# An attention-then-FFN kernel on one core: its head re-ordered (beta later, turn parts in own PSUM banks, dummy matmuls, a queue of squares, four begun FFN1 units)

## The chip, the cores and the metric

The kernel runs on one core of a Trainium2 chip. Its time is the device time of one execution in microseconds; the figure compared is the median of several runs. The profile is of one such execution. PE is TensorE, PEld its weight loads, DVE VectorE, ACT ScalarE, POOL GpSimd and SP SyncE, which here only starts transfers.

## What is computed

```
scores = q @ k^T / sqrt(64)                     # per batch (8) and head (12), 448 x 448
attn   = max(scores, 0)^2 / 448
x      = (attn @ v), heads side by side         # 3584 x 768
h      = x @ w_in                               # 3584 x 2048
g      = max(h, 0) + alpha * min(h, 0)
out    = g @ w_out                              # 3584 x 768, float32
```

Inputs are float32; the matmuls run in bf16.

## The kernel before, in words

Work is tiled by **quad**: four heads of one batch, so three quads (NG = 3) per batch and 24 in all. For each quad:

- `load_qk`, `load_v` (lines 86 to 99) bring q, k and v from HBM as bf16 through POOL's queue. The first quad's q and k come as float32 instead, on SP's and ACT's queues (lines 114 to 117), and are cast by DVE and ACT (line 123).
- `turn_pe` (133) transposes q and k with 14 PE transposes each into a PSUM bank (line 141) and copies them into tile `T` (144 on DVE, 146 on ACT). For the first quad the copy is cut into two parts for each of q and k. From quad 6 on `turn_dma` (149) is used: DVE permutes, a DMA transposes.
- `score_mm` (161) makes one of seven chunks j of scores: four matmuls of 64x64 weights and 448 columns, one for each quarter of the array, into a pair of banks (line 166).
- `relu` (172) takes a chunk out of PSUM as `rl`, on ACT (175) or DVE (177); the letter for each chunk is in the pattern string. `square` (180) multiplies `rl` by itself on DVE into `at` (182).
- `attnv` (185), A@V, accumulates seven squared chunks against v (28 matmuls, line 192) and writes the result, scaled, as `xT`: one half by ACT (199), one by DVE (200).

The FFN follows: `f1` (227) makes one of 16 units ff of a batch, six matmuls of 448 columns (215), then ACT makes `neg` = relu(-h) (223) and DVE gT = h + (1 - alpha) * neg (224), with `beta_sb` = 1 - alpha (line 128). `f2` (232) makes an output tile with 16 matmuls of 384 columns (237); ACT copies it out (239) and SP stores it.

The order of work on every engine is the order in which this Python code issues instructions: the schedule is manual, each engine runs its own list in order, and semaphores join them. PSUM is one tile of eight banks; `take_bank` and `take_pair` give the bank or the pair that was taken longest ago, and dependencies through PSUM are by bank. `rl` has 7 buffers, `at` 12, `neg` 3.

The head, lines 253 to 286, interleaves quads 0, 1 and 2 by hand in calls of `run`, which issues a group of score chunks with their relus and then all squares of the group. FFN1 of batch 0 then begins with two units begun on their first four matmuls (those that need only quads 0 and 1) before A@V of quad 2. Lines 300 to 327 mix FFN1 of batch 0, the scores of quads 3 to 5, and the first FFN2 units (which lack batch 1 and so take only c below 3). At line 349 two FFN1 units of batch 1 are begun ahead of A@V of quad 5. `burst` (338) is the later pattern: three chunks, A@V of an earlier quad, three chunks, then squares.

## Time and profile before

| what | value |
|---|---|
| median of 14 runs | 398.73 us (397.14 to 400.15) |
| the profiled execution | 397.89 us, span 396.1 us |
| PE busy | 376.2 us, 95% of the span |
| DVE busy | 265.7 us, 67% |
| ACT busy | 207.4 us, 52% |
| first 28 us: PE / DVE / ACT busy | 14.2 / 17.5 / 16.8 us |
| 28 to 73 us: PE / DVE / ACT busy | 42.7 / 33.4 / 28.2 us |
| 73 to 140 us: PE / DVE / ACT busy | 67.0 / 47.4 / 35.4 us |
| moved by DMA in the first 28 us | 190 GB/s |

The span is the time from the first to the last instruction on the core; the execution's own time has 1.8 us more around it. A timeline row gives start and duration of a run of like instructions on one engine, and in brackets the idle time of that engine just before, with what ended it. A matmul's duration runs from issue to the end of its pipeline, so neighbours overlap; the distance between starts is what a stream of them costs.

### The profile page before, as it was taken

How to read it: one execution, taken by the hardware profiler on the slowest of the kernel's cores; microseconds unless marked ns; L12 is line 12 of the kernel's file. 1: busy time of each engine (PE TensorE's matmuls, PEld its weight loads, DVE VectorE, ACT ScalarE, POOL GpSimd, SP SyncE). 2: the span in 40 equal slices, each digit the busy share in tenths (PEclk: the TensorE clock that was granted, in tenths of full speed). 3: DMA queues.
4: the chain of work that ended last, by engine and by line, in shares of the span. 5: the costliest groups of instructions: out<-in, count | busy, mean ns of one | idle time of the engine just before them, and what ended most of it. 6: DMA issues, size and time to landing. Idle time of an engine off the chain costs nothing.

```text
span 396.1 us, 7881 instructions
## 1 busy us (share of the span) xinstructions
PE 376.2 (95%) x3192; PEld 213.3 (54%) x3192; DVE 265.7 (67%) x419; ACT 207.4 (52%) x332; POOL 65.5 (17%) x97
## 2 busy tenths in 40 slices
PE   0779999999999999999999999999999999999996
PEld 0434445455566556654665546654555555655564
DVE  1896876774778687878756787777756786736400
ACT  2695666543565454655544555565444655534311
POOL 7558204240202022102202022020200000000000
PEclk9999999999999999999999999999999999999999
DMA  9999999699495749381975419690742302120023
GB/s 179 188 204 202 205 204 197 87 177 159 102 169 84 95 73 158 89 153 4 164 147 96 101 18 167 120 166 2 127 97 61 88 1 67 42 60 2 10 70 82
DMA packets 71909, 43.75 MB, mean 110 GB/s; under 512 B 38208, under 2 KB 71872, under 8 KB 71872
## 3 DMA queue, kind: packets, MB, share of 16 engines
q0 software_dynamic: 27312, 23.04, 40.7%
q1 hardware_dynamic: 44128, 19.65, 24.1%
q8 instruction: 25, 0.41, 0.4%
q10 hardware_dynamic: 432, 0.56, 0.4%
q14 instruction: 12, 0.10, 0.1%
HBM read 47.00 MB, written 11.01 MB: 146 GB/s over the span
## 4 chain that ended last, share of the span: by engine, by line
PE 87%; DVE 5%; ACT 4%; DMA 2%; issue 1%; ACTq 0%; SPq 0%
PE psum L237 37%; PE psum L215 36%; PE psum L166 7%; PE psum L192 6%; DVE at L182 3%; ACT rl L175 2%; DMA alpha_sb<-in_moe_alpha_dram 2%; PE psum L141 1%; DVE rl L177 1%; ACT xT L199 1%; DVE T L144 1%; DVE gT L224 0%; ACT neg L223 0%; DVE xT L200 0%; ACT osb L239 0%
## 5 line engine op out<-in xcount | busy, mean ns | idle before, releaser
L237 PE MATMUL psum<-w_out_sb,gT 128*128 128x384 bf16 (+2 forms) x912 | 150.7, 323 | 0.2
L215 PE MATMUL psum<-xT,w_in_sb 128*128 128x448 bf16 x768 | 148.7, 353 | 1.3 <-ACT xT L199 1.3
L237 PEld LDWEIGHTS <-gT 128*128 128x128 bf16 x912 | 87.6, 98 | 61.4 <-issue 6.7
L215 PEld LDWEIGHTS <-w_in_sb 128*128 128x128 bf16 x768 | 74.1, 98 | 72.3 <-issue 4.1
L224 DVE SCALAR_TENSOR_TENSOR gT<-neg,beta_sb,psum 128x448 bf16<-128x448 f32 x128 | 84.5, 679 | 41.3 <-ACT neg L223 40.8
L223 ACT ACTIVATE neg<-psum 128x448 f32<-128x448 f32 x128 | 69.5, 545 | 71.0 <-PE psum L215 66.7
L175 ACT ACTIVATE rl<-psum 128x896 bf16<-128x896 f32 x120 | 103.2, 922 | 2.0 <-PE psum L166 2.0
L182 DVE TENSOR_TENSOR at<-rl 128x896 bf16<-128x896 bf16 x168 | 94.2, 619 | 6.2 <-ACT rl L175 6.0
L239 ACT COPY osb<-psum 128x384 f32<-128x384 f32 (+2 forms) x57 | 27.0, 473 | 99.4 <-PE psum L237 96.0
L177 DVE TENSOR_SCALAR rl<-psum 128x896 bf16<-128x896 f32 x48 | 52.1, 1086 | 36.6 <-PE psum L166 36.6
L91 POOL DMA_DIRECT2D qraw<-in_q_dram x24 | 17.2, 718 | 200.3 <-DVE perm L152 177.2
L166 PE MATMUL psum<-T 64*64 64x448 bf16 x672 | 45.6, 361 | 4.8 <-ACT rl L175 1.6
L192 PE MATMUL psum<-at,vraw 64*64 64x448 bf16 x672 | 37.5, 350 | 0.6 <-DVE gT L224 0.5
L166 PEld LDWEIGHTS <-T 64*64 64x64 bf16 x672 | 20.7, 106 | 23.4 <-issue 14.4
L192 PEld LDWEIGHTS <-vraw 64*64 64x64 bf16 x672 | 24.7, 106 | 10.2 <-issue 2.8
L200 DVE TENSOR_SCALAR xT<-psum 128x448 bf16<-128x448 f32 x24 | 15.0, 624 | 12.9 <-ACT rl L175 7.1
L98 POOL DMA_DIRECT2D vraw<-in_v_dram x25 | 18.0, 721 | 1.3 <-DMA w_in_sb<-in_moe_w_in_dram 0.8
L91 POOL DMA_DIRECT2D kraw<-in_k_dram x24 | 17.3, 723 | 3.2 <-DVE gT L224 0.9
L199 ACT ACTIVATE xT<-psum 128x448 bf16<-128x448 f32 x24 | 13.1, 545 | 4.9 <-PE psum L192 4.9
L141 PE MATMUL psum<-ident,qraw 128*64 128x128 bf16 x84 | 4.5, 252 | 9.0 <-DVE qraw L123 5.9
L108 POOL DMA_DIRECT2D w_in_sb<-in_moe_w_in_dram x16 | 10.0, 628 | 7.9 <-DMA w_in_sb<-in_moe_w_in_dram 2.4
L152 DVE COPY perm<-qraw 128x896 bf16<-128x896 bf16 x18 | 11.0, 612 | 0.0
(17 smaller groups left out, 35.7 us busy)
## 6 DMA issues: line engine op xcount, KB each, us to landing
out_dram<-osb SPq DMA_DIRECT2D x110, 96.0 KB, 2.3
vraw<-in_v_dram POOLq DMA_DIRECT2D x25, 224.0 KB, 7.1
qraw<-in_q_dram POOLq DMA_DIRECT2D x24, 224.0 KB, 4.7
kraw<-in_k_dram POOLq DMA_DIRECT2D x24, 224.0 KB, 6.5
w_in_sb<-in_moe_w_in_dram POOLq DMA_DIRECT2D x16, 192.0 KB, 9.0
w_out_sb<-in_moe_w_out_dram POOLq DMA_DIRECT2D x2, 1536.0 KB, 18.1
qfirst<-in_q_dram SPq DMA_DIRECT2D x1, 448.0 KB, 4.4
kfirst<-in_k_dram ACTq DMA_DIRECT2D x1, 448.0 KB, 4.7
```

Source lines behind the costliest of these rows:

```text
L91: nc.gpsimd.dma_start(out=t.rearrange("p m j d -> p m (j d)"), in_=flat[:, 2 * g:2 * g + 2])
L98: nc.gpsimd.dma_start(out=t.rearrange("p m j d -> p m (j d)"), in_=flat[:, 2 * g:2 * g + 2])
L166: nc.tensor.matmul(ps[64 * c:64 * c + 64, r, :S], t[64 * r:64 * r + 64, 1, j, 64 * c:64 * c + 64], t[64 * r:64 * r + 64, 0, :, 64 * c:64 * ...
L175: nc.scalar.activation(rl, ps[:, :, :S], ACTF.Relu)
L177: nc.vector.tensor_scalar(rl, ps[:, :, :S], 0.0, None, ALU.max)
L182: nc.vector.tensor_tensor(a, rl, rl, ALU.mult)
L192: nc.tensor.matmul(ps[64 * s:64 * s + 64, r, :S], vv[64 * r:64 * r + 64, s, j, :], a[64 * r:64 * r + 64, s], start=(j == 0), stop=(j == NJ ...
L215: nc.tensor.matmul(ps, w_in_sb[:, km // 2, km % 2, bass.ts(ff, 128)], xT[b][:, km // 2, km % 2, :], start=(km == 0), stop=(km == KM - 1))
L223: nc.scalar.activation(neg, ps, ACTF.Relu, scale=-1.0)
L224: nc.vector.scalar_tensor_tensor(gT[b // 2][:, ff, (b % 2) * S:(b % 2) * S + S], neg, beta_sb[:, ff:ff + 1], ps, ALU.mult, ALU.add)
L237: nc.tensor.matmul(ps, gT[sb][:, ff, bass.ts(c, 128)], w_out_sb[:, hf, ff, lo:hi], start=(ff == 0), stop=(ff == KF - 1))
L239: nc.scalar.copy(o[:, lo:hi], ps)
```

## The change

- Beta is made by DVE in the middle of quad 2 instead of at the start.
- In `turn_pe` each part of a cut turn takes a bank of its own. For quad 0 the first part of k is copied by DVE instead of ACT, and k's cast is cut in two.
- 36 matmuls of the identity by itself, into bank 7, are issued on PE before the first casts; their result is not read.
- `run` is split in two: `sc` issues scores and relus and puts the chunks in a list `late`; `sq(k)` issues the squares of the oldest k. In the head the calls are set anew by hand, and the D (DVE) relus of quads 1 and 2 come at later chunks. From quad 3 to 5 the squares stay in the list, and each FFN1 unit issues one behind its own DVE step.
- For quads 0 and 1 ACT writes both halves of `xT` in one instruction of 896 columns.
- The first FFN2 unit is issued ahead of A@V of quad 3.
- Four FFN1 units instead of two are begun around A@V of quad 5: two ahead of it and two behind it. `prepare` for quads 6 to 8 comes after the unit of the same number instead of before.

The core of the diff:

```diff
     load_v(0)
+    warm = psum[:, 7, :128]
+    for _ in range(36):
+        nc.tensor.matmul(warm, ident, ident, start=True, stop=True)
-    for name, eng in (("q", nc.vector.tensor_copy), ("k", nc.scalar.copy)):
+    for name, eng, cut in (("q", nc.vector.tensor_copy, ((0, NJ),)), ("k", nc.scalar.copy, ((0, 2), (2, NJ)))):
...
-    nc.vector.tensor_scalar(beta_sb, alpha_sb, -1.0, 1.0, ALU.mult, ALU.add)
...
-            ps = take_bank().bitcast(BF16)
             src = raw.pop((n, name))
             for lo, hi, eng in (cuts, cuts_k)[i]:
+                ps = take_bank().bitcast(BF16)
...
+        if n < 2:
+            nc.scalar.activation(xT[b][:, g], ps[:, :, :S], ACTF.Copy, scale=out_scale)
+            return
...
+    late = []
+    def sc(chunks):
+        for n, j, eng in chunks:
+            late.append((n, j, relu(score_mm(n, j), eng)))
+    def sq(k=99):
+        for g in late[:k]:
+            square(*g)
+        del late[:k]
     def run(chunks):
+        sc(chunks)
+        sq()
...
                                        neg, beta_sb[:, ff:ff + 1], ps, ALU.mult, ALU.add)
+        sq(1)
...
-    turn_pe(0, ((0, 4, "D"), (4, NJ, "D")), ((0, 2, "A"), (2, NJ, "D")))
-    run(ch(0, 0, 3))
+    turn_pe(0, ((0, 4, "D"), (4, NJ, "D")), ((0, 2, "D"), (2, NJ, "D")))
+    sc(ch(0, 0, 4))
+    sq(3)
     load_qk(3)
-    run(ch(0, 3, 5))
+    load_v(3)
+    sc(ch(0, 4, 6))
     turn_pe(1)
-    run(ch(0, 5, 7))
-    load_v(3)
+    sc(ch(0, 6, 7))
+    sq(4)
...
-    run(ch(1, 0, 2))
+    sc(ch(1, 0, 3, "AAA"))
     attnv(0)
...
-    run(ch(1, 2, 4))
+    sq(2)
+    sc(ch(1, 3, 4))
     turn_pe(2)
-    run(ch(1, 4, 7))
+    sq(1)
+    sc([(1, 4, "D"), (1, 5, "A"), (1, 6, "A")])
+    sq(2)
     load_w_out(0)
-    run(ch(2, 0, 2))
+    sc(ch(2, 0, 2, "AA"))
+    sq(2)
     attnv(1)
...
-    run(ch(2, 2, 7))
+    sc(ch(2, 2, 4, "AAAAAAA"))
+    nc.vector.tensor_scalar(beta_sb, alpha_sb, -1.0, 1.0, ALU.mult, ALU.add)
+    sq(3)
+    sc(ch(2, 4, 7, "AAAAADA"))
+    sq()
...
-    run(ch(4, 2, 5))
-    attnv(3)
+    sc(ch(4, 2, 5))
+    sq()
     f2(0, 0, 0)
+    attnv(3)
...
-    for ff in range(2):
+    for ff in range(4):
         ps = take_bank()[:, :S]
         f1_mm(ps, 1, ff, range(4))
         early.append(ps)
-    attnv(5)
+        if ff == 1:
+            attnv(5)
```

## The prediction

> **What bounds the kernel now.** I read the slices first, then the timelines of VectorE (DVE) and TensorE (PE) over the first 80 us, then one matmul group by form in two windows.

> From the page, the span in 40 slices of 9.9 us:

> ```profile
> PE   0779999999999999999999999999999999999996
> DVE  1896876774778687878756787777756786736400
> ```

> After slice 3 PE is never below nine tenths, so nothing but matmul work sets the time there. The loss is in the first three slices (0, 7, 7), where DVE is at 8 and 9. The change must be priced there: what ends the time when PE is short of work?

> VectorE's timeline (start, duration, what, and in brackets its idle time before):

> ```profile
> 5.17 0.63 DVE L123 CAST qraw<-qfirst 128x896 bf16<-128x896 f32 x1 [5.17 <-DMA qfirst<-in_q_dram]
> 9.05 0.17 DVE L128 TENSOR_SCALAR beta_sb<-alpha_sb 128x16 f32<-128x16 f32 x1 [3.25 <-DMA alpha_sb<-in_moe_alpha_dram]
> ...
> 10.17 0.36 DVE L144 COPY T<-psum 128x384 bf16<-128x384 bf16 x1 [0.62 <-PE psum L141]
> 11.66 0.49 DVE L144 COPY T<-psum 128x640 bf16<-128x640 bf16 x1 [1.13 <-PE psum L141]
> 12.50 1.09 DVE L177 TENSOR_SCALAR rl<-psum 128x896 bf16<-128x896 f32 x1 [0.34 <-PE psum L166]
> 13.51 2.76 DVE L182 TENSOR_TENSOR at<-rl 128x896 bf16<-128x896 bf16 x5
> ...
> 29.89 0.63 DVE L182 TENSOR_TENSOR at<-rl 128x896 bf16<-128x896 bf16 x1 [0.18 <-ACT rl L175]
> ```

> Two phases. From 5.80 to 12.50 DVE idles 5.3 us: 3.25 behind beta, which waits for alpha's load, then 2.1 on cold, serialized transposes. From 12.50 to 30.52 it idles 0.18 us: here DVE is the bound, down to the last square that A@V of quad 2 needs.

> PE's timeline:

> ```profile
> 5.85 0.64 PE L141 MATMUL psum<-ident,qraw 128*64 128x128 bf16 x8 [5.85 <-DVE qraw L123]
> 9.60 0.53 PE L141 MATMUL psum<-ident,qraw 128*64 128x128 bf16 x6 [3.11 <-DVE T L144]
> ...
> 31.72 2.05 PE L215 MATMUL psum<-xT,w_in_sb 128*128 128x448 bf16 x10 [0.63 <-ACT xT L199]
> ...
> 54.91 1.51 PE L192 MATMUL psum<-at,vraw 64*64 64x448 bf16 x26 [0.47 <-DVE gT L224]
> ...
> 72.83 7.35 PE L215 MATMUL psum<-xT,w_in_sb 128*128 128x448 bf16 x38 [0.62 <-ACT xT L199]
> ```

> The 3.11 us are the bank: the second part of q's turn writes the bank that DVE still has to read. The last two rows are the two later stalls the change touches.

> The score matmul by form from 9 to 12 us (count, busy us, mean ns, idle before):

> ```profile
> L166 PE MATMUL psum<-T 64*64 64x448 bf16 x8 | 1.0, 578 | 0.0
> ```

> and from 16 to 24 us:

> ```profile
> L166 PE MATMUL psum<-T 64*64 64x448 bf16 x36 | 2.9, 359 | 3.1 <-ACT rl L175 1.6 <-DVE T L144 1.3 <-DVE xT L200 0.2
> ```

> The same matmul is 220 ns longer early: 448 columns at half rate. The page's clock row shows 9 throughout, so this must be read from durations. Chunks of four are 0.37 us apart early and 0.19 later.

> **Part by part.** Time is measured to the last square of quad 2 (30.52 now); all PE work behind it moves with it.

> *Beta moved.* DVE's first T copy, ready to run when the first eight transposes end (6.49), ran at 9.13. It moves to 6.53. Beta itself (0.1 us in a queue) goes between squares near 20 us, when alpha (landed 9.03) is long there: no new wait.

> *Own banks.* q's 14 transposes now run through: at half rate they are 0.05 us apart (10 in 0.75, tail 0.3), so q ends at about 6.8 and k (its cast in two parts, about 5.8 and 6.5, from 0.94 whole) at 7.5. DVE copies: 6.53+0.42, +0.36, +0.25 for k's first part (0.37 on ScalarE, now on DVE; between 0.36 for 384 columns and its share of 0.42 for 512), giving 7.55, then +0.49 = 8.0. First score 7.6; half-rate score 0.37+0.21, so the first relu on ScalarE (ACT) starts at 8.2 (now 12.12) and DVE's relu at 8.5 (now 12.50).

> *Moved relus, xT halves and squares.* Spacing in a queue: ACT relu 0.81 (2.54 for 3, the last 0.92); square 0.535 (2.67 for 5); T copy 0.535; DVE relu 1.0. The 128x896 xT copy isn't in the trace: from 0.44 (half of it) to 0.88 (two halves); I take the relu's 0.81, the same shape from PSUM. Two xT halves of 0.54 leave DVE; ACT pays 2x0.37 more. In the new order xT of quad 1 is ACT's 16th step: 8.2+15x0.81 = 20.35. It needs the last square of quad 1, in front of which and with which DVE has 2 relus, 14 squares, 4 copies: 2.0+7.49+2.14 = 11.6, so 20.1, 20.2 complete; A@V's last matmuls 0.35, xT at 20.6 to 21.4. ACT's next relu ends at 22.35. DVE, done with beta and two squares at 21.3, idles 1.1. Then square 0.535, relu 1.0, four squares 2.14: 26.15. The gain is 30.52-26.15 = 4.4. The same summing of the 12.50 to 30.52 stretch (3 relus, 21 squares, 4 copies, 2 xT halves, 0.18 idle) gives 17.6 against 18.0 measured, so half of that shortfall is deducted: **4.2**. Bounds, 3.4 to 4.9: the hand-overs between ACT and DVE are now closer.

> *Dummy matmuls.* ident is ready at 1.31. No row shows this shape; the nearest is the half-width transpose, 0.05 us, twice for full width: 36x0.10 = 3.6, end near 5.2, 0.6 before q's cast is done; cost nothing. Cover lost if a pair costs over 0.125. [...] I take the row. The lower bound is a gain: at full rate soon, transposes 0.03 apart, 0.3 earlier. [...] Full rate from about 8.3 is my sum above; half rate until 12 costs 0.4 (A@V of quad 0, 28 matmuls, is 2.7 instead of 1.4 and partly hidden), until 15 costs 1.1. [...]

> *Squares queued apart, A@V(3) behind the first FFN2 unit.* Between 28 and 56 DVE has the same instructions; one square (0.535) now follows each gT step (0.60), together 1.135, one PE unit's 1.135: no pile-up, and eight banks cover a hiccup. The 0.47 at 54.91 (bank of the last gT) is passed by 16 FFN2 matmuls (2.7 us): gain **0.5**. Bounds -0.4 (a wait like the 0.43 at 42.19 comes up at one more turn) to +0.8.

> *Four units at A@V(5).* Two more begun units put eight matmuls (8x0.189 = 1.5 us) over the 0.62 wait for xT: gain **0.6**, 0 to 0.6. The earlier 0.63 at 31.09 stays, having two units still. Preparing a quad one unit later delays transposes needed 15 us on: nothing.

> *Queues.* POOL's DMA order is unchanged, and up to 36 us its issues wait for earlier landings, not for compute, so landings stay: kraw of quad 4 at 37.8 (turn now 44.9, then 40), w_out's first half 46.6 (56.4, then about 50), kraw of quad 5 48.9 (59.6, then 54). Margins over 2 us; they cap the gain near 7.

> Sum: 4.2+0.5+0.6 = 5.3. The profiled execution took 397.89 (span 396.1 plus 1.8); it becomes 392.6. The median 398.73 is 0.84 above it; I keep that: **393.4**.

> **Rivals.**
> 1. Everything falls well (clock up early, full hand-overs): 4.9+0.3+0.8+0.6 = 6.6, median 392.1. For: PE's own work before 26 us is some 12 us at full rate, not the bound. Against: the 1.1 idle already counted, landings.
> [...]
> 3. Squares queued apart make ACT and DVE wait alternately, later stalls return elsewhere: 2 to 2.5, about 396.4.
> 4. It doesn't do what it says: the head is bound by DVE's list anyway (16.5 us of squares, relus, copies), only beta's wait goes and returns on k's path: within 0.2% (0.8 us), about 398.3. Against: first relu starts 4 us earlier by a plain sum.
> 5. Slower: the 36 dummies write one bank and run one after another at the full 314 ns of the cold 128x128 rows: 36x0.314 = 11.3, end at 12.6, q's turn 6.8 late; 5.3 gained, net +1.5, median 400.2. It decides from (4.5+5.3)/36 = 0.27 us a dummy. Against: 10 such transposes took 0.75 in all, writing one bank.

> **How the numbers follow.** Likeliest case 0.62 (4.3 to 6.2 gained), rival 1 0.12, rival 2 0.13, rival 3 0.06, rival 4 0.03, rival 5 0.04. The likeliest case alone spans 392.5 to 394.4. Range for 8 in 10: 391.5 (rival 1 and a little under it) to 396.4 (rivals 2 and 3 in). Within 0.2% is what a measurement of this kernel can't tell from none: faster 0.93, same 0.03, slower 0.04.

> **What would show it.** Right: first T copy near 6.5, first ACT relu near 8.2, xT(1) near 20.6 with about 1 us of DVE idle behind it, last square of quad 2 near 26, no PE wait before A@V(3) or after A@V(5), span near 390.8. Wrong: dummies ending after 5.8; early scores at 578 ns beyond 12 us; PE waiting on a load from HBM; new idle on PE between 28 and 56 us above 0.5 in sum.

## The result and the profile after

The changed kernel takes 392.62 us in the median of 10 runs (391.26 to 401.93) against 398.57 us of 47 runs before; the ratio is 0.9851, with a 95% interval of 0.9831 to 0.9870. Forecast were 393.4, in 391.5 to 396.4. Two of these ten runs (397.82 and 401.93), and the two longest of the 22 with the late part undone below (401.17 and 401.86), are slow ones, over 1.5% above the fastest of their kernel; without them the two medians are 392.59 and 397.77. The profiled execution took 391.78 us with a span of 390.0, 6.1 less than that of before; its sum had been 5.3.

The slices of the kernel after:

```profile
PE   6779999999999999999999999999999999999996
DVE  3978866855778777868756687878756786735300
```

The slices were 9.9 us and are 9.75 now. PE's row looks nearly the same, because the dummies (3.64 us) count as busy and because a busy digit doesn't tell half rate from full; the gain must be read from the timelines. VectorE's (start, duration, what, idle before):

```profile
6.42 1.28 DVE L147 COPY T<-psum 128x512 bf16<-128x512 bf16 x4 [0.51 <-PE psum L144]
7.99 1.09 DVE L180 TENSOR_SCALAR rl<-psum 128x896 bf16<-128x896 f32 x1 [0.28 <-PE psum L169]
...
22.41 0.63 DVE L185 TENSOR_TENSOR at<-rl 128x896 bf16<-128x896 bf16 x1 [1.09 <-ACT rl L178]
22.95 1.08 DVE L180 TENSOR_SCALAR rl<-psum 128x896 bf16<-128x896 f32 x1
23.95 2.22 DVE L185 TENSOR_TENSOR at<-rl 128x896 bf16<-128x896 bf16 x4
...
81.14 0.62 DVE L155 COPY perm<-qraw 128x896 bf16<-128x896 bf16 x1 [3.11 <-DMA T<-perm]
```

The four T copies run in one piece from 6.42, DVE's first relu is at 7.99 (it was 12.50), the idle 1.09 stands where the sum had put 1.1, and the last square ends at 26.17 (forecast 26.15; it was 30.52). The last row is new and was not forecast: 3.11 us in which DVE waits for a DMA transpose. PE's timeline:

```profile
1.36 3.64 PE L123 MATMUL psum<-ident 128*128 128x128 bf16 x36 [1.36 <-POOL ident masks.py:199]
5.96 0.58 PE L144 MATMUL psum<-ident,qraw 128*64 128x128 bf16 x14 [0.96 <-DVE qraw L127]
...
10.77 0.58 PE L144 MATMUL psum<-ident,kraw 128*64 128x128 bf16 x14 [0.51 <-DMA kraw<-in_k_dram]
...
27.24 2.05 PE L229 MATMUL psum<-xT,w_in_sb 128*128 128x448 bf16 x10 [0.62 <-ACT xT L205]
...
43.72 0.57 PE L169 MATMUL psum<-T 64*64 64x448 bf16 x8 [0.27 <-DVE T L147]
...
52.33 1.52 PE L195 MATMUL psum<-at,vraw 64*64 64x448 bf16 x28
...
66.73 16.82 PE L229 MATMUL psum<-xT,w_in_sb 128*128 128x448 bf16 x88
```

The 36 dummies end at 5.0, before q's cast. FFN1 goes on behind xT of quad 2 at 27.24 instead of 31.72. The waits at A@V(3) and behind A@V(5) are gone (the last two rows have none), and the 0.43 at a score in the same stretch too; 0.27 at a T copy is new. The last row runs to 83.5 in one piece: in this execution PE did not feel DVE's wait of 3.11.

### The profile page after: what moved, and what is told of

Same layout as the page of the kernel before. It is cut to its first block, busy times and chain, and to the rows that moved or that the text cites. A ratio compares the mean times of both kernels' runs of the same rounds, so it can differ in the third digit from the quotient of the medians.

```text
span 390.0 us, 7956 instructions
## 1 busy us (share of the span) xinstructions
PE 378.3 (97%) x3228; PEld 215.7 (55%) x3228; DVE 263.6 (68%) x418; ACT 207.4 (53%) x332; POOL 65.6 (17%) x97
## 4 chain that ended last, share of the span: by engine, by line
PE 87%; ACT 4%; DVE 4%; DMA 2%; issue 1%; POOL 1%; ACTq 0%; POOLq 0%
PE psum L252 38%; PE psum L229 36%; PE psum L169 7%; PE psum L195 6%; ACT rl L178 3%; DVE at L185 2%; DMA kraw<-in_k_dram 2%; PE psum L144 1%; DVE T L147 1%; ACT xT L205 1%; DVE rl L180 1%; DVE gT L238 0%; POOL vraw L98 0%; ACT osb L254 0%; POOL qraw L91 0%
## 5 line engine op out<-in xcount | busy, mean ns | idle before, releaser
L229 PEld LDWEIGHTS <-w_in_sb 128*128 128x128 bf16 x768 | 74.2, 98 | 71.8 <-issue 4.4
L169 PE MATMUL psum<-T 64*64 64x448 bf16 x672 | 44.7, 355 | 3.4 <-ACT rl L178 1.3
L169 PEld LDWEIGHTS <-T 64*64 64x64 bf16 x672 | 20.9, 105 | 21.0 <-issue 14.5
L206 DVE TENSOR_SCALAR xT<-psum 128x448 bf16<-128x448 f32 x22 | 13.7, 625 | 14.3 <-PE psum L195 7.2
L205 ACT ACTIVATE xT<-psum 128x448 bf16<-128x448 f32 x22 | 12.0, 544 | 5.4 <-PE psum L195 5.4
L155 DVE COPY perm<-kraw 128x896 bf16<-128x896 bf16 x18 | 11.0, 610 | 0.0
```

Source lines behind the costliest of these rows:

```text
L155: nc.vector.tensor_copy(p[:, i], raw.pop((n, name)).rearrange("p s j d -> p j s d"))
L169: nc.tensor.matmul(ps[64 * c:64 * c + 64, r, :S], t[64 * r:64 * r + 64, 1, j, 64 * c:64 * c + 64], t[64 * r:64 * r + 64, 0, :, 64 * c:64 * ...
L229: nc.tensor.matmul(ps, w_in_sb[:, km // 2, km % 2, bass.ts(ff, 128)], xT[b][:, km // 2, km % 2, :], start=(km == 0), stop=(km == KM - 1))
```

## The experiments

Kernels whose name begins with a are the kernel after with one thing taken back or added; those with b are the kernel before with one thing added. All were timed in five rounds beside the kernel before. The kernel after was not timed again with them, so a difference from its 392.62 carries the spread of its own ten runs.

### The parts one at a time

**No dummies.**

```diff
-    warm = psum[:, 7, :128]
-    for _ in range(36):
-        nc.tensor.matmul(warm, ident, ident, start=True, stop=True)
```

> The kernel after without its 36 dummy matmuls, which leave no result. My sum (the vector engines' lists bind once they have started): half rate until 12 to 15 us costs 0.8 to 1.5 us through the turns and A@V of quad 0, so 393.4 to 394.1, with early score matmuls near 578 ns. Rival, the rate doesn't matter because PE has slack: within 0.3 of 392.6. Rival, the rate is the main term: 395.5 or more.

Measured: 392.04 (391.89 to 392.12), if anything faster than the 392.62 with them. That is neither what I expected nor a tie I could explain: the early scores did run at half rate, as PE's score matmuls from 5 to 9 us show (count, busy us, mean ns, idle before),

```profile
L166 PE MATMUL psum<-T 64*64 64x448 bf16 x16 | 1.6, 557 | 0.0
```

and DVE's first relu came 0.63 later (8.62 for 7.99). FFN1 went on at 27.59, only 0.35 later than with dummies. The head had lost something and the median hadn't, so something behind the head had to take it back. What the dummies are worth is settled below.

**Beta first again.**

```diff
     for n in range(1, NG):
         load_qk(n)
         load_v(n)
+    nc.vector.tensor_scalar(beta_sb, alpha_sb, -1.0, 1.0, ALU.mult, ALU.add)
...
-    nc.vector.tensor_scalar(beta_sb, alpha_sb, -1.0, 1.0, ALU.mult, ALU.add)
     sq(3)
```

> The kernel after with beta made on DVE before the first T copies again. My sum: the first T copy goes from 6.42 back to about 9.2 and all behind it follows, +2.4 to +2.8, so about 395.2; DVE shows 3 us idle on alpha. Rival, the landing of quad 1's k (10.73, on the chain of the kernel after) is what holds the head: the delay is half absorbed, +1.0 to +1.6, about 394.0.

Measured: 396.05 (394.31 to 396.50), 3.4 more than the kernel after; its profiled execution 394.31, 2.5 more than the profiled one of after. Nothing is absorbed; the rival on k's landing falls.

```profile
8.94 0.17 DVE L132 TENSOR_SCALAR beta_sb<-alpha_sb 128x16 f32<-128x16 f32 x1 [3.12 <-DMA alpha_sb<-in_moe_alpha_dram]
9.03 1.27 DVE L148 COPY T<-psum 128x512 bf16<-128x512 bf16 x4
```

The same 3.1 us as before the change are back, and the T copies with them (9.03 for 6.42). In this profile PE was busy for only 0.73 us from 6.83 to 10.24 and ran at half rate from there to 13.66, so part of the cost can be the rate that the dummies had brought.

**One bank again.** In `turn_pe`, `take_bank` stands outside the loop over the parts.

> The kernel after with both parts of a cut turn in one bank again. At full rate the wait for the first copy of q is about 0.45 us and another for k, of which the first delays the first score: +0.4 to +0.9 by my sum, 393.0 to 393.5. Rival, the wait of 3.11 us in the kernel before was beta's and not the bank's, so nothing is left of it: within 0.2.

Measured: 392.68 (392.57 to 393.49), 0.06 above the median of after, which misses my 393.0 to 393.5 and meets the rival's number, but 0.9 to 1.4 above the profiled and the quickest executions of that kernel (391.3 to 391.8). Its timeline shows two waits of the expected kind, 0.52 and 0.43, each behind a T copy:

```profile
7.19 0.53 PE L144 MATMUL psum<-ident,qraw 128*64 128x128 bf16 x6 [0.52 <-DVE T L147]
...
8.36 0.74 PE L144 MATMUL psum<-ident,kraw 128*64 128x128 bf16 x10 [0.43 <-DVE T L147]
```

So of the 3.11 us before the change about 0.5 was the bank and the rest beta (beta late on the kernel before, below, shows the same 0.52); what the bank is worth in the median isn't settled by this run, since the rate rose late in its profiled execution too (its first 20 scores took 1.99, as they did without dummies).

**The part from 28 us on as before.** All lines from the third FFN1 unit to the first FFN2 unit with c = 3 are those of the kernel before.

> The kernel after with all from 28 us on as before: squares in groups, A@V(3) ahead of the first FFN2 unit, two begun units at A@V(5). My sum: +1.1 (0.5 and 0.6), with waits of about 0.5 ahead of A@V(3) and 0.6 after A@V(5) back, 393.7. Rival, the queue of squares itself costs or gains elsewhere: +0.3 or less, or +1.6 or more.

Measured: 398.19, and from 394.70 to 401.86 over 22 runs: 5.6 lost where I had said 1.1, nearly the whole gain of the change. This is the surprise of the study. The expected waits were there (0.47 ahead of A@V(3), 0.62 behind A@V(5)), but so was this, from DVE's and then PE's timeline:

```profile
77.61 0.68 DVE L238 SCALAR_TENSOR_TENSOR gT<-neg,beta_sb,psum 128x448 bf16<-128x448 f32 x1 [0.46 <-ACT neg L237]
85.69 0.62 DVE L155 COPY perm<-qraw 128x896 bf16<-128x896 bf16 x1 [7.39 <-DMA T<-perm]
86.22 0.61 DVE L155 COPY perm<-kraw 128x896 bf16<-128x896 bf16 x1
86.75 4.22 DVE L238 SCALAR_TENSOR_TENSOR gT<-neg,beta_sb,psum 128x448 bf16<-128x448 f32 x7
```

```profile
84.78 1.63 PE L252 MATMUL psum<-w_out_sb,gT 128*128 128x384 bf16 x9
87.48 0.34 PE L252 MATMUL psum<-w_out_sb,gT 128*128 128x384 bf16 x1 [1.07 <-DVE gT L238]
88.07 0.34 PE L252 MATMUL psum<-w_out_sb,gT 128*128 128x384 bf16 x1 [0.26 <-DVE gT L238]
```

`turn_dma` of quad 8 needs a third `perm` buffer where the pool has two. It must wait until the DMA transpose of quad 6 has read the first. DVE runs its list in order, so seven gT steps stand behind that copy; eight banks cover some of it, and then PE takes one FFN2 matmul per gT step, 0.59 us apart instead of 0.17.

**Beta late, on the kernel before.**

```diff
-    nc.vector.tensor_scalar(beta_sb, alpha_sb, -1.0, 1.0, ALU.mult, ALU.add)
...
-    run(ch(2, 2, 7))
+    run(ch(2, 2, 4))
+    nc.vector.tensor_scalar(beta_sb, alpha_sb, -1.0, 1.0, ALU.mult, ALU.add)
+    run(ch(2, 4, 7))
```

> The kernel before with beta alone moved behind four chunks of quad 2. My sum: the first T copy 2.6 us earlier, but the turn stays cold and in one bank, so the wait for the second part of q stays at about 0.5; all behind it moves by 2.5, and 396.1 comes out. Rival, the head is bound by DVE's list from 12.5 on or by landings: 1.3 or less gained, 397.3 or more.

Measured: 395.82 (395.10 to 396.66), against 398.79: 3.0 gained from one moved line, half of the whole. The wait at q's second part is down to the bank's share:

```profile
6.98 0.53 PE L140 MATMUL psum<-ident,qraw 128*64 128x128 bf16 x6 [0.52 <-DVE T L143]
```

DVE's first relu is 2.62 earlier (9.88 for 12.50), but the profiled execution gained only 1.39 (396.50): PE ran at half rate from 15.12 to 18.54, through A@V of quad 0.

**Dummies alone, on the kernel before.** The three lines of the first diff, added.

> The kernel before with the 36 dummy matmuls alone. My sum: DVE waits for alpha until 9 us whatever PE does, then the cold turn (2.1 us of DVE idle between 9.2 and 12.5) shrinks by about half, if the rate is still full at 9.6 after 3 us of idle PE: 0.8 to 1.2 gained, 397.5. Rival, the rate is lost again in those 3 us: within 0.2 of before. Rival, the rate is the main term of the change: 3 or more gained.

Measured: 399.22 (397.33 to 401.30), ratio 1.0008 (0.9988 to 1.0029): nothing that can be told from none. The first rival, the rate lost again, holds in kind, though the median is 0.43 up where it said within 0.2. PE stood from 6.8 to 11.2 and the rate was lost in that time; these are windows of 3.41 us (length, PE, PEld, DVE, ACT, POOL busy, then PEclk, the granted clock):

```profile
4.24:7.65 3.41, 1.07 (x19) 0.79 (x18) 0.95 (x1) 0.94 (x1) 2.97 (x5) 1.00 1.39 206
7.65:11.06 3.41, 0.00 (x0) 0.00 (x0) 0.42 (x2) 0.00 (x0) 1.85 (x3) 0.50 1.28 194
11.06:14.48 3.42, 2.83 (x36) 1.62 (x36) 1.32 (x4) 1.14 (x2) 1.87 (x4) 0.50 1.26 196
14.48:17.89 3.41, 3.34 (x44) 1.81 (x39) 3.41 (x7) 2.96 (x5) 1.42 (x3) 0.50 1.10 165
```

Its DVE timeline also has beta at 10.64 where the profile of before has 9.05: alpha's 8 KB landed 1.6 us later, and the execution took 399.38, 1.5 more than that of before. DVE's first relu is 1.59 later, so that is all alpha's. In four profiles with beta first it came at 8.94, 9.05, 9.53 and 10.64: alpha's landing varies between executions and, while beta stands first, goes into the time.

**The late part alone, on the kernel before.**

> The kernel before with only the part from 28 us on changed (squares queued, FFN2 unit ahead of A@V(3), four begun units). My sum: 1.1 gained, 397.5. Rival, the later stalls come from the late head and have gone with it: within 0.3 of before here, while they don't come back in the kernel after with this part undone.

Measured: 397.06, 1.73 gained; ratio 0.9956 (0.9941 to 0.9970). The gain is there without the early head, above the 1.1 of the sum.

**The front alone, with the old lists.** Beta late, own banks, cut cast, k's first part on DVE and dummies; relus, squares and xT halves as before.

> The kernel before with beta late, own banks, k's first part on DVE, k's cast cut and the dummies, but with the old lists of relus, squares and xT halves, and the old part from 28 us on. My sum: the first relu comes near 8 us instead of 12.1, 4 us earlier, and DVE's list of 18.0 us behind it stays: 3.7 to 4.2 gained, 394.6. With the lists as changed worth 0.2 to 0.5 more. Rival, the old lists waste the early start on landings or hand-overs: 2.5 or less gained, 396 or more, so that the new lists are worth 1.5 or more.

Measured: 394.83, 3.96 gained, inside my interval. But its profile says that I had the parts wrong: DVE's first relu is at 7.87, 4.6 earlier than before, and FFN1 goes on behind xT(2) at 28.75, only 3.0 earlier. The old lists lose 1.7 of the start:

```profile
16.39 0.62 DVE L203 TENSOR_SCALAR xT<-psum 128x448 bf16<-128x448 f32 x1 [0.41 <-PE psum L195]
17.73 0.62 DVE L185 TENSOR_TENSOR at<-rl 128x896 bf16<-128x896 bf16 x1 [0.72 <-ACT rl L178]
```

With squares in groups and xT's half on DVE, DVE waits for A@V(0) and then for the relus that ACT could start only behind its own half. The new lists get FFN1 to 27.24: they are worth 1.5, not the 0.4 of the sum. Part of this is the rate, though. PE's wait for the T copies behind five squares (1.31 us, ending at 12.80) left it busy for 1.67 us of 3.42 (9.27 to 12.69), and A@V(0) ran at half rate:

```profile
12.69:16.10 3.41, 3.30 (x36) 1.68 (x40) 3.28 (x6) 1.31 (x2) 1.64 (x3) 0.50 1.18 175
```

```profile
13.55 2.76 PE L195 MATMUL psum<-at,vraw 64*64 64x448 bf16 x28
```

In the kernel after it took 1.78. The one execution of six at full granted clock took 394.29, 0.54 below their median, so the lists' own worth and the rate's are not separated.

### The perm buffer

Two findings asked for one cause: no dummies cost nothing, and the late part undone cost 5.6. My theory: both kernels meet the same wait at quad 8's permutation, the more the earlier the head. The wait at that copy in the profiles with the new late part seemed to speak for it: 0.31 with beta first, 0.86 with one bank, 1.06 without dummies, 3.11 in the kernel after, in the order in which their heads get earlier.

The profiles say more than that. The room from the issue of quad 6's transpose to the moment DVE is ready for quad 8's copy doesn't depend on the head: it is 7.1 to 7.2 us in all profiles with the old late part and 6.1 to 6.2 in all with the new, which has DVE there sooner. What differs is how long the transpose takes to land, and each wait is, to about 0.1, that time less the room: 6.4, 7.0, 7.2 and 9.2 us in the four just named, 14.5 with the late part undone. These are the issue and the landing in the kernel before, the kernel after and with the late part undone:

```profile
L154 SPq DMA_TRANSPOSE T<-perm x1: 1407/1407/1407, 75.8 to 75.8; - x1
DMA to landing us min/median/max: 6.4/6.4/6.4
```

```profile
L157 SPq DMA_TRANSPOSE T<-perm x1: 1407/1407/1407, 71.8 to 71.8; - x1
DMA to landing us min/median/max: 9.2/9.2/9.2
```

```profile
L157 SPq DMA_TRANSPOSE T<-perm x1: 1407/1407/1407, 71.1 to 71.1; - x1
DMA to landing us min/median/max: 14.5/14.5/14.5
```

The test is a third buffer:

```diff
-    perm_pool = ctx.enter_context(tc.tile_pool(name="perm", bufs=2))
+    perm_pool = ctx.enter_context(tc.tile_pool(name="perm", bufs=3))
```

> The kernel after with a third perm buffer, so that the permutation of quad 8 need not wait for the transpose of quad 6 to have read its buffer. My theory: the 3.11 us in which DVE stands at that copy go; PE didn't wait for it in the profiled run, so the median is that of the kernel after's undisturbed executions, 391.3 to 391.9, and those of 395 to 402 that it had among ten don't come. Rival, those come from elsewhere: median 392.6 and a spread of several us again.

> The kernel after with all from 28 us on as before, and a third perm buffer. My theory: undoing that part costs only its two PE waits, 1.1, and the rest of its 398.2 was DVE standing 7.4 us at quad 8's perm copy: 392.6 to 393.2 and a narrow spread. Rival, the old order of squares is what costs 4 us or more once the head is early: 396.5 or more, still wide.

> The kernel after with a third perm buffer and without the dummy matmuls, which leave no result. My theory: with the perm wait out of the comparison the dummies show what they are worth in the head, 0.3 to 0.7: this is slower than the same kernel with dummies by that. Rival, they are worth nothing: within 0.15 of it. Second rival, they cost: this one is faster by 0.3 or more, as the plain comparison without a third buffer suggested.

Measured side by side: the kernel after with three buffers 391.37 (391.32 to 391.44), ratio 0.9818 (0.9796 to 0.9839); with the late part undone besides 392.87 (392.78 to 393.07); without dummies 391.84 (391.76 to 391.96).

The second is the clean case: one buffer takes 5.3 us from 398.19, and the spread shrinks from 7.2 (22 runs) to 0.3 (4 runs). The order of squares had no part in it. What is left against the first, 1.50, is the late part's own worth. For the kernel after, the buffer gives 1.25 in the median and 0.42 in the profiled executions; the intervals of the two ratios touch (0.9831 to 0.9870, 0.9796 to 0.9839), so that size is uncertain. Four of its ten runs had been at 393.4 to 401.9, and the seventeen runs of the four kernels with three buffers hold together within 0.4 each; that those four met the perm wait is likely, but none of them was profiled. The three longest had granted clocks of 0.994, 0.989 and 0.986, so PE lost its full rate somewhere in them, as it did behind the stall with the late part undone. The dummies, finally, are worth 0.47 here, with no overlap between the runs, which the plain comparison had turned round. DVE's list with the third buffer has no wait at the copy:

```profile
77.04 0.68 DVE L238 SCALAR_TENSOR_TENSOR gT<-neg,beta_sb,psum 128x448 bf16<-128x448 f32 x1 [0.43 <-ACT neg L237]
77.64 0.61 DVE L155 COPY perm<-qraw 128x896 bf16<-128x896 bf16 x1
78.17 0.61 DVE L155 COPY perm<-kraw 128x896 bf16<-128x896 bf16 x1
```

**Four begun units at A@V(2) as well.**

```diff
-    for ff in range(2):
+    for ff in range(4):
         ps = take_bank()[:, :S]
         f1_mm(ps, 0, ff, range(4))
         early.append(ps)
-    attnv(2)
-    for ff in range(2):
+        if ff == 1:
+            attnv(2)
+    for ff in range(4):
         f1_mm(early[ff], 0, ff, range(4, KM))
         f1_out(early[ff], 0, ff)
...
-    f1s(0, 2, 3)
...
-    f1s(0, 3, 5)
+    f1s(0, 4, 5)
```

> The kernel after with a third perm buffer and four FFN1 units begun around A@V(2), as at A@V(5), two ahead of it and two behind. My theory: the 0.62 us that PE waits for xT of quad 2 at 26.6 are covered by eight matmuls: 0.6 faster than with the third buffer alone, about 391.0. Rival, the wait turns up one step later, at the turn of quad 3, since its q and k land at about 27: within 0.15.

Measured: 391.70 (391.44 to 391.82), 0.3 slower than with the third buffer alone. The 0.62 at xT(2) is gone and this took its place:

```profile
26.01 3.20 PE L229 MATMUL psum<-xT,w_in_sb 128*128 128x448 bf16 x16
...
32.27 0.76 PE L169 MATMUL psum<-T 64*64 64x448 bf16 x12 [0.91 <-DVE T L147]
```

The wait did turn up one step later, as the rival had it, though not for a landing and at more than its 0.15: PE's turn of quad 3 is done in time, but its T copies stand on DVE behind four gT steps that all came at once. The same move that was free at A@V(5), where no turn follows, costs here.

The best version is the kernel after with a third perm buffer: 391.37 us, 7.2 below the kernel before timed beside it and 1.25 below the kernel after.

## Why the prediction was right, point by point

- *The head's sum* (4.2): FFN1 went on 4.48 earlier. The end points of the DVE and ACT lists fell within 0.2 us of the forecast (last square 26.17 for 26.15, xT(1) at 20.65 for 20.6). That the last square fell so close is partly luck: the start came 0.5 earlier than forecast (7.99 for 8.5), and the list from there took 18.18 where the sum had 17.65. (The sum's own terms from 22.35 on add up to 26.03 and not 26.15.) The rest of the error lies in the split: I gave 4.0 to the early start and next to nothing to the lists. The start gives 4.5, of which the old lists would have lost 1.5 (28.75 against 27.24), in part through the rate. I had summed the new lists in order, but never the old ones from the early start.
- *Beta moved* (2.6 of DVE's start): right, 2.61 at the first T copy and 2.5 in the profiled executions with and without it in the kernel after. In medians it is 3.0 and 3.4. I put the rest down to alpha's landing, which came as late as 10.6 in one profile and is in the time of every execution with beta first; that no profile of a median run shows it leaves this likely and not shown.
- *Own banks*: right in kind, 0.5 and 0.4 of wait, but the 3.11 us that I read as the bank's in the kernel before were mostly beta's; the size in the median stays between 0.1 and 1.4.
- *Dummies*. Their cost, by the transpose row 36x0.10 = 3.6, was measured as 3.64 with the end at 5.0, part of it at full rate (a dummy took 312 ns in the mean up to 4.4 us, 239 from 4.5). Rival 2 has 0.13 of the chances and a part in the range's 396.4; no run shows a term for it: in the kernel after the last dummy ended 0.96 ahead of q's first transpose, and the granted clock stayed at 1.00 from 4.45 on. Their worth is 0.47 in the finished kernel and nothing in the kernel before. With them the rate in the profile of the kernel after was full from the first transposes (14 in 0.58; 0.96 without dummies), not from 8.3 as I took it, and the half rate until 12 or 15 that I priced didn't come: it stayed full behind the window with quad 0's 28 transposes (4.45 to 7.86, PE busy for 2.20 us). That isn't so in every profile with dummies: with beta first and with the third buffer the first 14 transposes took 0.96 as well.
- *The late part* (1.1): mis-sized. 1.5 with three buffers and 1.7 on the kernel before. The two waits were 0.47 and 0.62 as priced; the third, 0.43 at a score in 42.19, I had entered as a risk and not as a gain.
- *"Preparing a quad one unit later delays transposes needed 15 us on: nothing"* is the step that failed. I asked when its product is needed, not what stands behind it on DVE. In the kernel before, the transpose of quad 6, issued at 75.8, landed 6.4 us later at 82.2, and quad 8's copy ran at 82.90: 0.7 of slack that no view calls a wait. The new late part took 0.9 of the room. The head took none, since it moves the transpose and the copy alike, but it brought the transpose nearer to loads that had not moved: quad 8's v landed at 74.1 in the kernel before, 1.7 us ahead of the transpose's issue, and also at 74.1 in the kernel after, 2.3 us behind it. In the nine profiles in which a wait, or a view of it alone, shows its landing, the transpose landed in 6.4 to 6.6 us where it was issued at 74.4 or later (three), and in 6.6 to 14.5 where it was issued at 71.1 to 73.6 (six). That the meeting with the loads is what makes it late was not tested. So the failed step has a second half, in *Queues*: I asked of landings only whether they hold up the turns, not what a transfer that does move would meet.
- *Sum and median*: 6.1 in the profiled executions against 5.3 of the sum, 5.95 in the medians: what the lists and the late part gave above the forecast, the perm wait took back in part. That 393.4 came within 0.8 of the median owes something to two errors of opposite sign.
- *Landings* from HBM stayed as said, within 0.2 us: k of quad 4 at 37.7 for 37.8, the first half of w_out at 46.5 for 46.6, k of quad 5 at 48.7 for 48.9. One got onto the chain: k of quad 1 landed at about 10.7, and its turn waited 0.51 for it. It cost little, since ACT had relus to do.
- Of the rivals, the slow one (dummies at 314 ns each) is refuted by the 3.64, and that stalls return elsewhere (rival 3) was truer than the chance I gave it: one did, at a place I hadn't looked at, in the kernel with the late part undone.

## What to carry to other kernels

When a stage is made earlier, list for every in-order engine the buffers that it reuses downstream, and how long before their reuse the reader now lands: a slack below a microsecond, 0.7 here, can become a wait (3.11 and 7.39), and no view shows it. Ask also which transfers move with the stage and which stay, and whether they now meet. A wide spread of one kernel's runs, where its neighbours hold within 0.4, can be the sign of a wait that depends on a landing; look for the copy at the head of the list that stopped. Compare single edits only with such a wait taken out, since it can turn a gain of 0.5 into a loss of 0.6.

## What the runs showed of the hardware

Apart from the very end of the span, PE's rate was lost in six of these profiles: for 3.41 us in five (with beta first again, with the late part undone, and on the kernel before with beta late, the front alone and the late part alone; mean granted clock 0.994 to 0.996) and for 10.24, three times that, with the dummies alone (0.986). The windows below are cut at the times at which the granted clock changed, in steps of 3.41. They come from four kernels; behind the first three the granted clock was 0.50 in the next window, behind the fourth, of the kernel before, it stayed at 1.00:

```profile
11.71:15.12 3.41, 1.46 (x36) 0.83 (x35) 3.41 (x7) 2.76 (x4) 1.75 (x4) 1.00 1.20 172
```

```profile
9.27:12.69 3.42, 1.67 (x36) 0.98 (x36) 3.42 (x8) 3.08 (x5) 1.88 (x3) 1.00 1.26 202
```

```profile
87.00:90.41 3.41, 1.68 (x5) 0.48 (x5) 3.41 (x7) 2.18 (x4) 1.75 (x3) 1.00 1.27 167
```

```profile
15.10:18.50 3.40, 1.81 (x37) 0.88 (x37) 3.40 (x8) 2.78 (x4) 1.72 (x3) 1.00 1.20 191
```

The DMA transpose of quad 6, the same size in all kernels, took from 6.4 to 14.5 us to land where a profile shows it. It ran beside loads for later quads in the kernel before (6.4; issued at 75.8, loads at 75.5 to 76.9) as in the kernel after (9.2; issued at 71.8, loads at 71.5 to 72.9), and with the third buffer it was issued at 71.5 and landed in 6.6. What sets the time within this range wasn't tried and stays open. One thing to try is at hand: both kernels load quad 8's q, k and v twice, once after `turn_pe(5)` and once in `prepare(6)` (POOL issues q 24 times for the 23 quads that it loads). The v that is in flight when the transpose of quad 6 is issued in the kernel after belongs to the second, needless load.
